# Attention scores in 64 by 64 tiles of TensorE, each block of queries with its own keys

## The chip, the cores and the metric

One core of one Trainium2 chip. The metric is device microseconds of one execution; a kernel is run several times and the median is given. The core has five engines that run side by side and meet at semaphores: TensorE (PE, whose weight loads the profile lists as PEld), VectorE (DVE), ScalarE (ACT), GpSimd (POOL) and SyncE (SP, which here issues the DMAs).

## The reference

Three stages follow each other: sparse attention, a gated feed-forward layer ("moe") and a second one ("moe2"). The change is in the attention. Four batches, eight heads, 512 local and 32 global positions, head size 64:

```
s_ll = scale * q_l @ k_l.T            # 512 x 512, kept where |i - j| <= 32
s_lg = scale * q_l @ k_g.T            # 512 x 32
a_l  = softmax([s_lg, s_ll])
out_l = a_l @ [v_g, v_l]
out_g = softmax(scale * q_g @ [k_g, k_l].T) @ [v_g, v_l]
x = [out_g, out_l] -> 2176 x 512 -> moe -> moe2
```

A local query sees 65 local keys and all 32 global ones.

## The kernel before

The attention stage is written out by hand. It is cut into small tasks, each with an engine (or two to choose from), the tasks it needs, and the PSUM banks it takes. `ORDER` is one long string; each letter names a kind of task in `KINDS`, and the next task of this kind is put there. A `+1` behind the kind chooses the second engine. So the string is the instruction order of all engines at once: on each engine tasks run in the order of the string, and an engine whose next task is not ready waits. `keep_busy` adds matmuls of zeros behind the first PE tasks, in numbers given by a string of digits (19 calls in all).

The tasks of a pair of heads `n` (16 pairs) are:

- `qk`: loads of keys and queries on SP. The queries are loaded shifted by 32 positions, so that a block of 64 queries has its keys in a window of 128.
- `A`: 16 transposes of 64 by 64 on PE (L212); `Ak` and `Aq` copy the turned keys and queries out of PSUM, to `kst` and `qT`, on ScalarE or DVE (L235, L237).
- `At` (L293, L294): POOL copies each pair of blocks' next 64 keys behind its own 128, so that row r of `kst` holds 192 local keys; `Ag` (L287): POOL copies the 32 global keys behind them, four times. A row has 224 keys.
- `S`, twice for a pair (g = 0, 1), so 32 calls of `scores` in the stage: four matmuls of 128 queries (two blocks of 64) and 224 keys, for two query pairs and two heads; the heads lie in the two halves of the partitions. L314.
- `M` (DVE, L325): adds the mask, writes the negated scores and their minimum; `E` (ScalarE, L332): the exponential and its sum; `R`, `N` (POOL, L344 and L346): the division. Eight of `M` and `E` a pair.
- `C`: transposes of the weights (L212), copied out by `V`; `D`: the product with the values (L378 with the global, L382 with the local ones), both for two heads in the two column halves of PE; `Xc`, `Xh`, `Xl`: the result is copied and split in a high and a low part.

For every two pairs there are global queries as well (`GA`, L408; `GT`; `GO`, L454), for every batch the turning of the global keys and queries (`AG`, L478, `AGk`, `AGe`, `GG`). Between them stand the first matmuls of the next layer (`F`, `F2`, L650) and the conversion of its first weights (`Cq`, `Cf`, `Ch`, `Cl`).

A PE matmul has a tile shape, the rows and columns of the array that it takes: 64 by 128 for the scores and the 64 by 64 transposes, 128 by 64 for `D`, `GA`, `GO` and `GG`, 128 by 128 for `AG`, `F`, `F2` and `keep_busy`.

Behind attention the two layers run from a list that a planner in the kernel puts in order when it is built; the change does not touch it.

Of the kernel before, what the change touches and what calls it, by code (L numbers as in the profile page):

```python
# [21 lines left out]
def tile_attn_moe_moe2(  # L22
# [69 lines left out]
    mask = e_p.tile([128, 224], F32, name="mask")  # L92
    mask7 = e_p.tile([128, 224], F32, name="mask7")
# [4 lines left out]
    def setup():  # L98
        nc.gpsimd.memset(ident, 1.0)
        nc.gpsimd.affine_select(out=ident, in_=ident, pattern=[[-1, 128]], compare_op=ALU.is_equal,  # L100
                                fill=0.0, base=0, channel_multiplier=1)
        keep_busy(0, 7)
        nc.vector.memset(qgbd, 0.0)
        for t in (vg, vgb):
            nc.vector.memset(t, 0.0)

        nc.gpsimd.memset(mask, 0.0)
        m = mask[:, 0:192]
        nc.gpsimd.affine_select(out=m, in_=m, pattern=[[1, 192]], compare_op=ALU.is_ge,
                                fill=NEG, base=0, channel_multiplier=-1)  # L110
        nc.gpsimd.affine_select(out=m, in_=m, pattern=[[-1, 192]], compare_op=ALU.is_ge,
                                fill=NEG, base=64, channel_multiplier=1)

        nc.gpsimd.tensor_copy(mask7, mask)
        nc.gpsimd.memset(mask7[64:96, 128:192], NEG)
        nc.gpsimd.memset(mask7[96:128, 64:128], NEG)


    XF = {}
# [90 lines left out]
    def transpose_half(out, src, j):  # L210
# [7 lines left out]
    KINDS = ("qk A gk w Ak+1 Aq At Cq AG AGk Ag S M E AGe GG GA GGe+1 Cf GM R vg v vgb N Ak GE GR GN C V "
             "Ch GT GV D AGk+1 Aq+1 GO Xc GXc+1 Xd GV+1 Cl Xc+1 GXh+1 Xh Xh+1 Xl GXl V+1 Ch+1 GXd F_v "
             "F_g GXc Ft Fg Fp Fh Fl Fh+1 GXl+1 F2 Fy Fy+1 GXh Xl+1").split()  # L220
    ORDER = "abcdaefgchaijkllmkmmmmmmnnnnibopedcnqgnramsnntbskfelfhluvammmmmmmmwnxnnngyybizgsAnBCkfDEDEnqsslmmFnnGcHm"
    ORDER += "muwnntlbnIemnnJAyayKmmmigDEDoBslkCEalpLkmmmmmnMnnumnGnnnmNmnnnIyywOwPbaQRDznESfOqDlsuyETUlmmmmmmmmnnnnyI"
    ORDER += "DDnrnnEngVVkWdtLXbwAlMefIusYZcmvOlmmQmgnUnnBbmmmM01ayymzhsnnf2DDnEEnCdqlssscgVGwnIUHamnmlummMVtnSAnyWyk1"
    ORDER += "YmmmmnnnnnUb0zxKOZaDXQiiDBlEjhul3Immm4kCyg1mmmmmVb5nnnnnnnnDsLefyEGwuoRTHl6DqEpy2lmOnmnmymnSgsbekkrfImmm"
    ORDER += "nnmDZwOadaE7nWns1tsYcDlgLEQVlmmAmmbInnnnu3eRmmyyqkmmKlUnn2D0wvVRBnEtDC4mmm00USWgVncm5GnuEhnnlOwy1s8xiHbd"
    ORDER += "7msmmyAnIefaDnnsmEn13nBCilsnMDjou0LyyEmmmml4wOGnnnngphmmmZkPrIDmw5Dnnnn0uEEbUlYssImeOMOmmmfUn2SqskyyVaDD"
    ORDER += "sZaELgEtlFQQlMImnnVkmmmm9TAnmBmmbVCnM2nnn!!xzufnnn#ylb!y!emmnnnSm#n6Km#gkwvwDDXX17gnZlOOddulmm$UIqWyymmm"
    ORDER += "mmmtGD1nnnnnnnnEu0P3ADVl45EL6lwIwmmnmnnmnyyBmmm7mNZnnnnDCuD!My!OREyXUGI%DU9PDEL$#X&VI2%9OMTOMUZ!!$$O&&"
# [36 lines left out]
    def add_pair(n):  # L265
# [14 lines left out]

        def kst():
            if (b, hp) not in KST:
                KST[b, hp] = kst_p.tile([128, 4, 224], F32, tag="kst", name="kst")
            return KST[b, hp]

        def glob_keys():
            nc.gpsimd.tensor_copy(kst()[:, :, 192:224], GK[b, "kT"][:, hp:hp + 1, :].to_broadcast([128, 4, SG]))  # L287

        def keys():
            duplicate(("Ak", n), kst()[:, :, 0:128].rearrange("c r (j t) -> c r j t", j=2), R["pk"])  # L290

        def more_keys():
            nc.gpsimd.tensor_copy(kst()[:, 0:3, 128:192], kst()[:, 1:4, 0:64])  # L293
            nc.gpsimd.tensor_copy(kst()[:, 3, 128:192], kst()[:, 0, 0:64])  # L294

        def queries():
            R["qT"] = qk_p.tile([128, 4, 128], F32, tag="qT", name="qT")
# [1 line left out]
            duplicate(("Aq", n), dst, R["pq"])  # L299

        task(("A", n), "PE", [("qk", n)], qk, 2, ("Aq", n))
        task(("Ag", n), "POOL", [("AGk", b), lastu("GA", n - 2), agog("S", 2, 1)], glob_keys)
        task(("Ak", n), "DVE ACT", [("A", n), lastu("GA", n - 2), agog("S", 2, 1)], keys)
        task(("At", n), "POOL", [("Ak", n)], more_keys)
        task(("Aq", n), "ACT DVE",
             [("A", n), ("Ak", n), agog("S", 2, 1)], queries)

        def scores(g):  # L310
            p = both(("S", n, g))
            for pp in range(2):
                for h in range(2):
                    nc.tensor.matmul(p[:, h, 224 * pp:224 * pp + 224], lhsT=R["qT"][half(h), 2 * g + pp, :],  # L314
                                     rhs=KST[b, hp][half(h), 2 * g + pp, :], start=True, stop=True)

        def minimum(g, i):
            if "sm" not in R:
                R["sm"] = sm_p.tile([128, NB, 224], F32, tag="sm", name="sm")
# [20 lines left out]
        def normalise(g):  # L340
            i0, i1 = 4 * g, 4 * g + 4
            r, sm = R["rc"][:, i0:i1], R["sm"]
            eng = nc.gpsimd if ON["N", n, g] == "POOL" else nc.vector
            eng.tensor_tensor(out=sm[:, i0:i1, 0:192], in0=sm[:, i0:i1, 0:192],  # L344
                              in1=r.unsqueeze(2).to_broadcast([128, 4, 192]), op=ALU.mult)
            eng.tensor_tensor(out=R["sng"][:, i0:i1, :], in0=sm[:, i0:i1, 192:224],  # L346
                              in1=r.unsqueeze(2).to_broadcast([128, 4, SG]), op=ALU.mult)


# [1 line left out]
        def turn(g):  # L351
            p = both(("C", n, g))
            for k in range(4):
                for j in range(2):
                    transpose_half(p[:, j, 64 * k:64 * k + 64], R["sm"][half(j), 4 * g + k, 64 * j:64 * j + 128], j)
# [6 lines left out]

        task(("R", n), "DVE", [("E", n, 0, 3), ("E", n, 1, 3)], reciprocal)
        for g in range(2):
            task(("S", n, g), "PE", [("Aq", n), ("At", n), ("Ag", n)], lambda g=g: scores(g), 2, ("M", n, g, 3))
            for i in range(4):
                task(("M", n, g, i), "DVE",
                     [("S", n, g), agog("C", 2, 1)], lambda g=g, i=i: minimum(g, i))
                task(("E", n, g, i), "ACT", [("M", n, g, i)], lambda g=g, i=i: exponential(g, i))
            task(("N", n, g), "POOL DVE", [("R", n), agog("C", 2, g)], lambda g=g: normalise(g))  # L370
            task(("C", n, g), "PE", [("N", n, g)], lambda g=g: turn(g), 2, ("V", n, g))
            task(("V", n, g), "ACT DVE", [("C", n, g), ago("D", 1)], lambda g=g: turned(g))
# [25 lines left out]
    def add_glob(u):  # L398
# [73 lines left out]
    def add_batch(b):  # L472
# [31 lines left out]
        task(("AGk", b), "DVE ACT", [("AG", b, 0)] + prev(("Ag", HP * b - 1), ("GG", b - 1)), keys)  # L504
# [32 lines left out]
    def attention():  # L537
# [903 lines left out]
```

## Time and profile before

| | |
|---|---|
| median of three runs | 891.6 us (891.56 to 893.38) |
| profiled execution, its own time | 890.72 us |
| span of its instructions | 889.0 us |
| PE busy | 877.6 us (99%) |
| VectorE, ScalarE, POOL busy | 649.6, 490.8, 541.3 us |
| attention ends on PE at | 158.8 us |

The profile is of one execution. A row of the timeline gives where instructions start, in microseconds from the start of the span, and how long one or several of them take; ends of matmuls are modelled, starts are recorded. The span leaves out what lies before the first and behind the last instruction, 1.7 us here.

### The profile page before, as it was taken

What the parts mean: (1) busy time and instruction counts of PE and PEld (TensorE: products, weight loads), DVE (VectorE), ACT (ScalarE), POOL (GpSimd) and SP (SyncE); (2) the same over time, 40 slices, a digit from 0 to 9 for tenths busy, and PEclk for the clock granted to TensorE, in tenths of its full rate; (3) what the DMA queues carried; (4) which work ended last, traced back from release to release, by engine and by line L of the source; (5) the groups of instructions that cost most, each with busy time, mean ns of one, the idle gap of its engine ahead of it and who ended that gap; (6) DMA issues with size and microseconds to landing.
All of it is one profiled execution on the core that took longest, in us unless ns stands there. A gap on an engine that the chain in (4) does not pass through costs nothing.

```text
span 889.0 us, 17205 instructions
## 1 busy us (share of the span) xinstructions
PE 877.6 (99%) x6252; PEld 808.0 (91%) x6252; DVE 649.6 (73%) x1224; ACT 490.8 (55%) x1177; POOL 541.3 (61%) x550
## 2 busy tenths in 40 slices
PE   7999999999999999999999999999999999999998
PEld 6777888988999999999999999998989898989896
DVE  5777786779777888778778899777777777753434
ACT  6888886454435454455455678764445444544341
POOL 4798887699964386375374799564454436633231
PEclk9999999999999999999999999999999999999999
DMA  7777775577555646646546335664737374726283
GB/s 167 169 182 168 189 173 147 197 233 240 195 190 197 224 148 209 205 139 230 178 153 221 137 142 194 224 222 156 250 116 261 121 263 139 259 80 197 61 266 144
DMA packets 165334, 164.19 MB, mean 185 GB/s; under 512 B 81793, under 2 KB 143745, under 8 KB 165249
## 3 DMA queue, kind: packets, MB, share of 16 engines
q1 hardware_dynamic: 163824, 162.24, 57.8%
q8 instruction: 49, 0.80, 0.4%
q10 hardware_dynamic: 1424, 0.85, 0.3%
q14 instruction: 37, 0.30, 0.1%
HBM read 136.31 MB, written 26.74 MB: 183 GB/s over the span
## 4 chain that ended last, share of the span: by engine, by line
PE 94%; DMA 2%; SPq 1%; DVE 1%; ACT 0%; issue 0%; ACTq 0%; DVEq 0%
PE p L1127 37%; PE p L1232 21%; PE p L1018 15%; PE p L1084 8%; PE one L650 3%; PE pair L212 2%; PE pair L314 2%; PE one L378 1%; PE one L382 1%; DMA qs<-in_q_l 1%; PE one L454 1%; DMA gkq<-in_q_g 1%; PE one L408 1%; DMA vw<-in_v_l 0%; SPq L178 0%
## 5 line engine op out<-in xcount | busy, mean ns | idle before, releaser
L1127 PE MATMUL p<-xh,w 128*128 128x384 f32 (+1 forms) x992 | 258.3, 326 | 0.0
L1232 PE MATMUL p<-w,a 128*128 128x512 f32 x816 | 194.3, 391 | 0.0
L1232 PEld LDWEIGHTS p<-w,a 128*128 128x128 f32 x816 | 152.2, 188 | 29.9
L1127 PEld LDWEIGHTS p<-xh,w 128*128 128x128 f32 x992 | 176.9, 188 | 1.4
L1127 PE MATMUL p<-xl,w 128*128 128x384 f32 (+1 forms) x496 | 161.5, 326 | 0.0
L1139 ACT ACTIVATE b<-p 128x384 f32<-128x384 f32 (+1 forms) x144 | 68.0, 472 | 158.1 <-PE p L1127 153.7
L1018 PE MATMUL p<-a,w 128*128 128x384 f32 (+2 forms) x768 | 142.8, 334 | 0.0
L1048 POOL TENSOR_TENSOR a<-b,a 128x384 fp32r<-128x384 f32 (+1 forms) x58 | 62.0, 1068 | 117.9 <-ACT a L1046 76.6
L1018 PEld LDWEIGHTS p<-a,w 128*128 128x128 f32 x768 | 130.5, 188 | 2.8
L1242 DVE TENSOR_TENSOR y<-p,y 128x512 f32<-128x512 f32 x119 | 82.1, 690 | 65.3 <-PE p L1232 63.8
L880 POOL TENSOR_TENSOR w<-cx,w 128x256 fp32r<-128x256 f32 (+1 forms) x90 | 100.0, 1119 | 44.4 <-ACT w L879 38.9
L833 DVE TENSOR_TENSOR b<-p,b 128x384 f32<-128x384 f32 (+1 forms) x144 | 76.3, 531 | 64.2 <-PE p L1127 42.9
L1048 POOL TENSOR_TENSOR a<-s,a 128x384 fp32r<-128x384 f32 (+2 forms) x53 | 61.5, 1161 | 65.8 <-ACT a L1046 65.8
L1127 PE MATMUL p<-e,w 128*128 128x384 f32 (+1 forms) x528 | 101.3, 328 | 0.0
L1127 PEld LDWEIGHTS p<-xl,w 128*128 128x128 f32 x496 | 93.1, 188 | 1.5
L1127 PEld LDWEIGHTS p<-e,w 128*128 128x128 f32 x528 | 90.0, 188 | 1.0
L1027 DVE TENSOR_TENSOR y<-p,y 128x384 f32<-128x384 f32 (+2 forms) x116 | 62.5, 542 | 22.7 <-PE p L1018 21.3
L1084 PE MATMUL p<-xh,w 128*128 128x384 f32 (+1 forms) x256 | 72.6, 355 | 0.0
L1046 ACT ACTIVATE a<-s 128x384 fp32r<-128x384 f32 (+2 forms) x88 | 45.4, 516 | 47.0 <-DVE s L1070 45.9
L591 DVE SCALAR_TENSOR_TENSOR fl<-q,st 128x512 f32<-128x512 f32 x68 | 62.4, 918 | 9.8 <-ACT q L583 9.6
L595 DVE SCALAR_TENSOR_TENSOR cx<-fl,cx 128x512 uint32<-128x512 uint32 x68 | 65.9, 969 | 0.5
L332 ACT ACTIVATE sm<-sm,nb 128x224 f32<-128x224 f32 x128 | 60.0, 473 | 3.7 <-DVE nb L325 3.6
(153 smaller groups left out, 1512.9 us busy)
## 6 DMA issues: line engine op xcount, KB each, us to landing
e<-td SPq DMA_DIRECT2D x76, 384.0 KB
xh<-td SPq DMA_DIRECT2D x38, 384.0 KB
xl<-td SPq DMA_DIRECT2D x38, 384.0 KB
st<-in_moe_w_out SPq DMA_DIRECT2D x28, 512.0 KB
st<-in_moe_w_in SPq DMA_DIRECT2D x16, 512.0 KB
vw<-in_v_l SPq DMA_DIRECT2D x32, 224.0 KB
e<-td SPq DMA_DIRECT2D x20, 320.0 KB
st<-in_moe_w_gate SPq DMA_DIRECT2D x12, 512.0 KB
```

The source lines that it names most:

```text
L591: nc.vector.scalar_tensor_tensor(fl, q, TINY2, hw, op0=ALU.is_ge, op1=ALU.mult)
L595: nc.vector.scalar_tensor_tensor(x, fu, 0xC0000000, x, op0=ALU.bitwise_and, op1=ALU.bitwise_or)
L833: return lambda e: vec(e).tensor_tensor(out=out(), in0=a(), in1=b(), op=op)
L880: add(lo or [("POOL", PO(n))], 0, lambda e: vec(e).tensor_tensor(out=dst(1), in0=src(), in1=dst(0).bitcast(F32), op=ALU.subtract), r=[rd, ...
L1018: nc.tensor.matmul(ps.h[:, 0:n], lhsT=a.h[:, d], rhs=b.h[:, at:at + n], start=(i == 0 and j == 0), stop=(i == len(ws) - 1 and j == 2))
L1027: add("DVE", DV(n), lambda e: nc.vector.tensor_tensor(out=ya, in0=ps.h[:, 0:n], in1=ya, op=ALU.add), r=[ps], w=yt)
L1048: t.append(add(either(n), 0, lambda e: vec(e).tensor_tensor(out=dst(1), in0=get(), in1=dst(0).bitcast(F32), op=ALU.subtract), r=[v, (av[0] ...
L1084: nc.tensor.matmul(ps.h[:, 0:n], lhsT=a.h[:, d], rhs=b[:, c, c0:c0 + n], start=(c == 0 and j == 0), stop=(c == KD - 1 and j == 2))
L1127: nc.tensor.matmul(ps.h[:, 0:n], lhsT=w.h[:, 256 * a + 128 * c:256 * a + 128 * c + 128], rhs=xs[b][:, c, :], start=(start and c == 0 and j ...
L1139: add("ACT", AC(n), lambda e: nc.scalar.activation(out=dst.h[:, 0:n], in_=src.h[:, 0:n], func=AF.Copy), r=[sv], w=[dst])
L1232: nc.tensor.matmul(ps.h, lhsT=a.h[:, d], rhs=b.h, start=(i == 0 and q == 0), stop=(i == len(ws) - 1 and q == 2))
L1242: add("DVE", DV(512), lambda e: nc.vector.tensor_tensor(out=ya, in0=pa(), in1=ya, op=ALU.add), r=[ps], w=tok)
```

## The change

The scores are computed for blocks of 64 queries, each with its own 128 local keys and the 32 global keys. `kst` holds the 512 local keys once; the copies `At` and `Ag` are gone, and the global keys are read from where `AGk` puts them, which now has two buffers. A call of `scores` has 16 matmuls instead of 4: 64 queries each, of 128 columns or of 32, and for the last block, whose window wraps, two of 64. The output rows of the two blocks lie in the two halves of the PSUM partitions as before. A row of scores has 160 columns instead of 224, and the masks, minimum, exponential and division follow it. The order string is a new one, with other engines chosen for some tasks: 11 of 32 `V` on DVE (6 before), 7 of 16 `Aq` on DVE (4 before), 1 of 8 `GV` on DVE (4 before), 3 of 32 `N` on DVE (none before), 6 of 16 `Xl` on DVE (3 before). `keep_busy` gets 18 calls. On SP the second half of a batch's first global load comes before the loads of pair 1.

```diff
         for j in range(2):
+            m = mask[half(j), 0:128]
+            nc.gpsimd.affine_select(out=m, in_=m, pattern=[[1, 128]], compare_op=ALU.is_ge,
+                                    fill=NEG, base=0, channel_multiplier=-1)
...
-                KST[b, hp] = kst_p.tile([128, 4, 224], F32, tag="kst", name="kst")
+                KST[b, hp] = kst_p.tile([128, SL], F32, tag="kst", name="kst")
...
-        def glob_keys():
-            nc.gpsimd.tensor_copy(kst()[:, :, 192:224], GK[b, "kT"][:, hp:hp + 1, :].to_broadcast([128, 4, SG]))
-
         def keys():
-            duplicate(("Ak", n), kst()[:, :, 0:128].rearrange("c r (j t) -> c r j t", j=2), R["pk"])
-
-        def more_keys():
-            nc.gpsimd.tensor_copy(kst()[:, 0:3, 128:192], kst()[:, 1:4, 0:64])
-            nc.gpsimd.tensor_copy(kst()[:, 3, 128:192], kst()[:, 0, 0:64])
+            duplicate(("Ak", n), kst().rearrange("c (r j t) -> c r j t", j=2, t=64), R["pk"])
...
-        task(("Ag", n), "POOL", [("AGk", b), lastu("GA", n - 2), agog("S", 2, 1)], glob_keys)
         task(("Ak", n), "DVE ACT", [("A", n), lastu("GA", n - 2), agog("S", 2, 1)], keys)
-        task(("At", n), "POOL", [("Ak", n)], more_keys)
...
         def scores(g):
-            p = both(("S", n, g))
+            p, keys = both(("S", n, g)), KST[b, hp]
             for pp in range(2):
-                for h in range(2):
-                    nc.tensor.matmul(p[:, h, 224 * pp:224 * pp + 224], lhsT=R["qT"][half(h), 2 * g + pp, :],
-                                     rhs=KST[b, hp][half(h), 2 * g + pp, :], start=True, stop=True)
+                r = 2 * g + pp
+                for j in range(2):
+                    i = 2 * r + j
+                    for c0, c1, o in ((64 * i, 64 * i + 128, 0),) if i < NB - 1 else ((SL - 64, SL, 0), (0, 64, 64)):
+                        for h in range(2):
+                            nc.tensor.matmul(p[half(j), h, 160 * pp + o:160 * pp + o + c1 - c0], lhsT=R["qT"][half(h), r, half(j)],
+                                             rhs=keys[half(h), c0:c1], start=True, stop=True)
+                    for h in range(2):
+                        nc.tensor.matmul(p[half(j), h, 160 * pp + 128:160 * pp + 160], lhsT=R["qT"][half(h), r, half(j)],
+                                         rhs=GK[b, "kT"][half(h), hp, :], start=True, stop=True)
...
-            eng.tensor_tensor(out=sm[:, i0:i1, 0:192], in0=sm[:, i0:i1, 0:192],
-                              in1=r.unsqueeze(2).to_broadcast([128, 4, 192]), op=ALU.mult)
+            eng.tensor_tensor(out=sm[:, i0:i1, 0:128], in0=sm[:, i0:i1, 0:128],
+                              in1=r.unsqueeze(2).to_broadcast([128, 4, 128]), op=ALU.mult)
...
-            task(("S", n, g), "PE", [("Aq", n), ("At", n), ("Ag", n)], lambda g=g: scores(g), 2, ("M", n, g, 3))
+            task(("S", n, g), "PE", [("Aq", n), ("Ak", n), ("AGk", b)], lambda g=g: scores(g), 2, ("M", n, g, 3))
...
-            kT = GK[b, "kT"] = g_p.tile([128, HP, SG], F32, tag="gkT", name="gkT")
+            kT = GK[b, "kT"] = g_p.tile([128, HP, SG], F32, tag="gkT", name="gkT", bufs=2)
...
-        steady = iter("040202002030020013")
+        steady = iter("030042000024201")
```

## Rows read from the trace of the kernel before

**Rows 1.** The page's busy times: microseconds, share of the span, instructions.

```profile
PE 877.6 (99%) x6252; PEld 808.0 (91%) x6252; DVE 649.6 (73%) x1224; ACT 490.8 (55%) x1177; POOL 541.3 (61%) x550
```

**Rows 2.** Busy time by stretch: stretch, length, PE, PEld, DVE, ACT, POOL, clock, DMA.

```profile
0.00:30.00 30.00, 25.07 (x284) 19.74 (x286) 17.49 (x75) 21.52 (x67) 16.04 (x40) 1.00 0.72 166
30.00:90.00 60.00, 57.32 (x928) 46.02 (x926) 45.34 (x176) 50.46 (x164) 51.85 (x65) 1.00 0.73 177
90.00:158.80 68.80, 68.80 (x1068) 58.61 (x1065) 51.30 (x173) 53.21 (x170) 53.90 (x63) 1.00 0.67 167
158.80:889.00 730.20, 726.37 (x3985) 683.67 (x3984) 535.45 (x802) 365.62 (x777) 419.49 (x385) 1.00 0.56 188
```

**Rows 3.** Busy time of `keep_busy` alone (L157) on PE and PEld, one stretch.

```profile
0.00:30.00 30.00, 9.62 (x52) 7.94 (x52) 1.00 0.72 166
```

**Rows 4.** The chain that ended last: start, length, what.

```profile
42.18 3.75 DMA vw<-in_v_l
```

**Rows 5.** Timeline of PE behind 125 us: start, length, instructions.

```profile
127.74 1.03 PE L314 MATMUL pair<-kst,qT 64*128 64x224 f32 x8
128.60 0.41 PE L212 MATMUL pair<-ident,ks 64*128 64x64 f32 x8
...
134.18 1.78 PE L314 MATMUL pair<-kst,qT 64*128 64x224 f32 x16
135.90 1.09 PE L378 MATMUL one<-pt,vg 128*64 128x128 f32 x16
136.82 1.10 PE L382 MATMUL one<-pt,vw 128*64 128x64 f32 x32
137.75 1.03 PE L408 MATMUL one<-kst,qgbd 128*64 128x512 f32 x4
...
142.13 0.97 PE L314 MATMUL pair<-kst,qT 64*128 64x224 f32 x8
143.03 0.66 PE L454 MATMUL one<-gtl,vw 128*64 128x32 f32 x16
143.52 0.29 PE L454 MATMUL one<-gtl,vgb 128*64 128x32 f32 x4
...
144.32 1.03 PE L314 MATMUL pair<-kst,qT 64*128 64x224 f32 x8
145.28 1.09 PE L378 MATMUL one<-pt,vg 128*64 128x128 f32 x16
```

**Rows 6.** Timeline of PE from 59.3 to 60.4 us.

```profile
59.48 0.28 PE L382 MATMUL one<-pt,vw 128*64 128x64 f32 x2
59.59 0.27 PE L378 MATMUL one<-pt,vg 128*64 128x128 f32 x1
59.60 1.02 PE L382 MATMUL one<-pt,vw 128*64 128x64 f32 x27
```

**Rows 7.** Groups by line and shape up to 150 us: busy, mean ns, idle before.

```profile
L332 ACT ACTIVATE sm<-sm,nb 128x224 f32<-128x224 f32 x128 | 60.0, 473 | 3.7 <-DVE nb L325 3.6
L344 POOL TENSOR_TENSOR sm<-sm,rc 128x768 f32<-128x768 f32 x31 | 46.8, 1510 | 11.2 <-DVE rc L338 8.0 <-ACT xf L235 2.4 <-ACT pt L235 0.9
L325 DVE CUSTOM_DVE_ANT_0 sm<-pair,mask 128x224 f32<-128x224 f32 x128 | 42.6, 385 | 21.4 <-PE pair L314 16.0 <-PE pair L212 1.7 <-POOL sng L346 1.7
...
L235 ACT ACTIVATE pt<-pair 128x640 f32<-128x640 f32 x25 | 17.1, 701 | 7.4 <-PE pair L212 6.6 <-ACT sm L332 0.6
...
L235 ACT ACTIVATE qT<-pair 128x512 f32<-128x512 f32 x12 | 7.1, 592 | 0.6 <-DVE kst L237 0.6
...
L293 POOL COPY kst<-kst 128x192 f32<-128x192 f32 x16 | 6.7, 419 | 10.6 <-ACT kst L235 9.6 <-DVE kst L237 1.0
```

**Rows 8.** Timeline of all engines from 5 to 9.3 us.

```profile
6.35 0.59 ACT L235 ACTIVATE qT<-pair 128x512 f32<-128x512 f32 x1
...
7.39 1.44 PEld L314 LDWEIGHTS pair<-kst,qT 64*128 64x128 f32 x16 [0.26 <-POOL kst L287]
...
7.83 1.15 SPq L169 DMA_DIRECT2D gkq<-in_q_g  x2
```

More of the change, by code (lines that the diff above doesn't have):

```diff
@@ L91, in tile_attn_moe_moe2 @@
     ident = e_p.tile([128, 128], F32, name="ident")
-    mask = e_p.tile([128, 224], F32, name="mask")
-    mask7 = e_p.tile([128, 224], F32, name="mask7")
+    mask = e_p.tile([128, 160], F32, name="mask")
+    mask7 = e_p.tile([128, 160], F32, name="mask7")
     qgbd = e_p.tile([128, HP, 2, SG], F32, name="qgbd")
@@ L107, in setup @@
         nc.gpsimd.memset(mask, 0.0)
[L108 to L112, printed above, removed]
+        for j in range(2):
+            m = mask[half(j), 0:128]
+            nc.gpsimd.affine_select(out=m, in_=m, pattern=[[1, 128]], compare_op=ALU.is_ge,
+                                    fill=NEG, base=0, channel_multiplier=-1)
+            nc.gpsimd.affine_select(out=m, in_=m, pattern=[[-1, 128]], compare_op=ALU.is_ge,
+                                    fill=NEG, base=64, channel_multiplier=1)
         nc.gpsimd.tensor_copy(mask7, mask)
-        nc.gpsimd.memset(mask7[64:96, 128:192], NEG)
-        nc.gpsimd.memset(mask7[96:128, 64:128], NEG)
+        nc.gpsimd.memset(mask7[64:96, 64:128], NEG)
+        nc.gpsimd.memset(mask7[96:128, 0:64], NEG)
     XF = {}
@@ L217, in tile_attn_moe_moe2 @@
     LETTERS = ascii_letters + digits + "!#$%&()*+-./:;<=>?@[]^_{|}~"
[L218 to L227, printed above, removed]
@@ L228, in tile_attn_moe_moe2 @@
-    ORDER += "mmmtGD1nnnnnnnnEu0P3ADVl45EL6lwIwmmnmnnmnyyBmmm7mNZnnnnDCuD!My!OREyXUGI%DU9PDEL$#X&VI2%9OMTOMUZ!!$$O&&"
+    KINDS = ("qk A Ak+1 gk AG AGk Aq S M w E Cq AGe Cf GA GG vg v GGe R N GM GE C V+1 vgb GR Ch+1 GN V D "
+             "Cl GT Aq+1 GV Xc+1 AGk+1 GO GXc+1 Ak Xh+1 Xl GXh GXl Xc Xd Ch GXd F_v F_g GXc GXh+1 Ft "
+             "GV+1 Fg Xh Fp Fh Fl GGe+1 F2 Xl+1 GXl+1 Fy Fy+1 Fh+1 N+1 Fl+1").split()
+    ORDER = "abcdefghijdahjiiiiikekdklkmakbnnnicogkhiepqrlnkkiiikshiibkkktiucvgakiiukwxyxzkABCDkhiiiihikrEFkkkbatinku"
@@ new lines, in tile_attn_moe_moe2 @@
+    ORDER += "kiicGkoHuktuuxIDxDJjdvhhiiiiwkkkkKaLAbiiiMNHCErreOxinxPykkkkDQGmRhInlbipiSTtEnucakHiihuOsikkxLUkyPTVixia"
+    ORDER += "oiFSyhbkkkkOtEiuciiiTgPrnukxhvWnqkSkOXiiniPDikYkkjxhyWiiddwiikZRkkhnrbtEikkkkuuNgTjzxiiAkioyVSxhCavklkeX"
+    ORDER += "DiiiKktehiuumkkGiE0wna1UFiLAkiikxYxCX2DybkkkSGnnntcrrXgIb3ThZc4PVpgoaiiluhiikkkksEiUuiiin5Txxa3DLnPDJhvk"
+    ORDER += "6RhkiiiiiEdFkkwktbiuqJkkkNiiAu0WXrgnCObYkxNeWDjHPd2kkxOznhTD4orkPitKiiuuEhiviV5iiiaxekkkkXDx6lmkGDWIQRhn"
+    ORDER += "nakkJkhiEw0iiiitBLiikkkikbrnuuxcAW2gnCDhMTV4kxXkTFDbriiiiBkOhkQptEa7iiiiukckFoSHGOxuI8aykk9!Sk#hxyLOkkTE"
@@ L230, in task @@
+    ORDER += "iiiivrkY9hkkjqbikk8ikStQuuNw8RzkAiHi#CXr$kbkxc8TVTDHOtPx%Ph#DWii6uhoikkkikiiiikkkE&0ktxvuuGDW2Ixw4jhLDAi"
+    ORDER += "ChkSiiiir5Ekkk(iiikMrxxkkky8JD8t&8TVTG&EI#$OOxxQyD!9L9EYZSS!8VTT39$$39"
     def task(name, engine, needs, work, banks=0, until=None):
@@ L310, in scores @@
         def scores(g):
-            p = both(("S", n, g))
+            p, keys = both(("S", n, g)), KST[b, hp]
             for pp in range(2):
-                for h in range(2):
-                    nc.tensor.matmul(p[:, h, 224 * pp:224 * pp + 224], lhsT=R["qT"][half(h), 2 * g + pp, :],
-                                     rhs=KST[b, hp][half(h), 2 * g + pp, :], start=True, stop=True)
+                r = 2 * g + pp
+                for j in range(2):
+                    i = 2 * r + j
[6 more added lines that the diff above has]
+                                         rhs=GK[b, "kT"][half(h), hp, :], start=True, stop=True)
         def minimum(g, i):
             if "sm" not in R:
-                R["sm"] = sm_p.tile([128, NB, 224], F32, tag="sm", name="sm")
+                R["sm"] = sm_p.tile([128, NB, 160], F32, tag="sm", name="sm")
                 R["sng"] = sm_p.tile([128, NB, SG], F32, tag="sng", name="sng")
@@ L325, in minimum @@
             nc.vector.tensor_tensor_reduce(
-                out=R["sm"][:, x], in0=both(("S", n, g))[:, h, 224 * pp:224 * pp + 224],
+                out=R["sm"][:, x], in0=both(("S", n, g))[:, h, 160 * pp:160 * pp + 160],
                 in1=mask7 if 2 * g + pp == 3 else mask, scale=-scale, scalar=3.0e38,
@@ L343, in normalise @@
             eng = nc.gpsimd if ON["N", n, g] == "POOL" else nc.vector
-            eng.tensor_tensor(out=sm[:, i0:i1, 0:192], in0=sm[:, i0:i1, 0:192],
-                              in1=r.unsqueeze(2).to_broadcast([128, 4, 192]), op=ALU.mult)
-            eng.tensor_tensor(out=R["sng"][:, i0:i1, :], in0=sm[:, i0:i1, 192:224],
+            eng.tensor_tensor(out=sm[:, i0:i1, 0:128], in0=sm[:, i0:i1, 0:128],
+                              in1=r.unsqueeze(2).to_broadcast([128, 4, 128]), op=ALU.mult)
+            eng.tensor_tensor(out=R["sng"][:, i0:i1, :], in0=sm[:, i0:i1, 128:160],
                               in1=r.unsqueeze(2).to_broadcast([128, 4, SG]), op=ALU.mult)
@@ L354, in turn @@
                 for j in range(2):
-                    transpose_half(p[:, j, 64 * k:64 * k + 64], R["sm"][half(j), 4 * g + k, 64 * j:64 * j + 128], j)
+                    transpose_half(p[:, j, 64 * k:64 * k + 64], R["sm"][half(j), 4 * g + k, 0:128], j)
             for j in range(2):
@@ L407, in scores @@
                 lq = qgbd[:, 2 * up + e].rearrange("c h r -> c (h r)")
-                nc.tensor.matmul(one(("GA", u))[half(e)], lhsT=lq, rhs=KST[b, 2 * up + e][:, :, 0:128],
+                nc.tensor.matmul(one(("GA", u))[half(e)], lhsT=lq, rhs=KST[b, 2 * up + e],
                                  start=True, stop=True)
@@ L503, in add_batch @@
         task(("AG", b, 0), "PE", [("gk", b, 0)], lambda: turn(0), 1, ("AGe", b))
-        task(("AGk", b), "DVE ACT", [("AG", b, 0)] + prev(("Ag", HP * b - 1), ("GG", b - 1)), keys)
+        task(("AGk", b), "DVE ACT", [("AG", b, 0)] + ([("S", HP * (b - 1) - 1, 1), ("GG", b - 2)] if b > 1 else []), keys)
         task(("AG", b, 1), "PE", [("gk", b, 1), ("AG", b, 0)], lambda: turn(1))
```

## The prediction

> **What bounds the kernel now.** I read the page's busy times first. TensorE is busy 99% of the span and no other engine reaches 75% [rows 1]. That is an average over two stages, so the second view is the table of stretches [rows 2]. The change touches only the attention stage, which ends at 158.8 us. In the stage behind it PE is busy 726.37 of 730.20 us in code that stays as it is; it will start earlier or later and keep its length. Inside attention there are three parts. Up to 30 us PE is idle for 4.93 us, and 9.62 us of its busy time are the dummy matmuls of `keep_busy` [rows 2, 3]; that is a ramp in which ScalarE (21.52 of 30 us) and the loads set the pace. From 30 to 90 us PE idles 2.68 us. From 90 us on it does not idle at all. So whatever the new score matmuls cost more or less on PE is paid in full behind 90 us, and nearly so before; whatever the other engines gain counts only up to 90 us. [...] The third view is the chain that ended last: before 90 us it leaves PE for loads, for instance 3.75 us for a value window at 42.18 us [rows 4], so not every idle microsecond is an engine's fault.
>
> **What a score call costs on PE.** The timeline of PE gives starts [rows 5]. An f32 matmul leaves two records, so `scores(g)` with four matmuls is a group of 8. The group of 16 takes 135.90 - 134.18 = 1.72 us to the next group, the group of 8 takes 145.28 - 144.32 = 0.96; both come from and go to another tile shape. The difference, 0.76 us, is one body without its edges: 4 pairs of records of 224 columns, 0.19 us a pair, the two heads side by side in the two row halves. Edges: the group of 8 at 127.74 goes on to transposes, which have its own shape (64 rows by 128 columns), and takes 0.86, so leaving for another shape costs 0.10; the one at 142.13 comes from transposes and takes 0.90, so entering from another shape costs 0.06.
>
> Rates of 64-column weights stand in the same rows: 16 records of 128 columns in 136.82 - 135.90 = 0.92 us, less the 0.05 of entering 0.109 a pair; 32 records of 64 columns in 137.75 - 136.82 = 0.93 us, 0.058 a pair; 16 records of 32 columns in 143.52 - 143.03 = 0.49 us, 0.061 a pair. So 32 columns cost what 64 do, which counts against the separate matmul over 32 global keys.
>
> **The new body.** A call now has 16 matmuls, 32 records: for each of two query pairs and each half j, two passes over 128 local columns and two over 32 global ones, for both heads. One half's passes take 2 x 0.109 + 2 x 0.058 = 0.334 us. No row shows a 64 by 64 tile, so this is bounded from both sides. If the four tiles run at once, j = 0 and j = 1 overlap and a call takes 2 x 0.334 = 0.668, which is 0.088 less than now, 32 times: -2.8 us. If the halves run one behind the other it takes 1.336: +18.6 us. The row nearest to the question is at 59.48 us [rows 6]: the two column halves of the output matmuls had got out of step, and one half starts L382 at 59.48, 0.11 us before the other half starts its last L378, though all of L378 is written ahead of L382. So the column halves have queues of their own and pass each other; the row halves run side by side in [rows 5]. A 64 by 64 tile is both at once, and I take 0.668. [...]
>
> **Edges.** Transposes share the present shape and nothing shares the new one. Decoding both order strings and putting the dummy matmuls where the digits put them, PE changes shape 106 times in attention now and 121 times then. 15 x (0.10 + 0.06) = +2.4 us; entering with weights half as wide may be cheaper, so +1.5 is the lower end. Body and edges together: -0.4 us. The fewer columns are paid back in edges.
>
> **The other engines.** The two key copies and the copy of the global keys leave POOL (the largest, L293, is 6.7 us in all), normalising shrinks from 768 to 512 columns at 1510 ns, and 3 of 32 normalisations go to DVE [rows 7]. POOL is not on the chain, so that is nothing by itself, except at the very start: the first scores wait for the last of those copies until 7.39 us, while the queries, which they still need, are there at 6.35 + 0.59 = 6.94 [rows 8]. -0.45 us. The masks' extra two selects on POOL lie in its idle time ahead of the first copy. On ScalarE copies of 640 and 512 columns take 701 and 592 ns, 0.85 ns a column, so an exponential over 64 columns fewer loses 0.054 of its 473 ns [rows 7]. In the ramp ScalarE is the engine with the least room, and it takes about 24 exponentials there (three pairs): -1.3 us; none if loads pace it, -2.0 if waits shorten too. DVE's minimum (385 ns) loses columns too, but the order gives DVE five more of the copies behind C and three more of the query copies (and three fewer behind GT); I count nothing for it. The dummy matmuls go from 19 to 18 calls: -0.2. Between 30 and 90 us I give back half of the 2.68 us of idle time, -1.3 (bounds: none, all), because scores no longer wait for POOL and ScalarE has some 4 us less to do there.
>
> The new order moves loads on SP: the second half of the global load now stands ahead of pair 1's keys and queries, and that is 1.15 us of issue [rows 8]. Pair 1 comes later by as much; behind it wait its transposes on PE and its two copies on ScalarE, which is still at pair 0's exponentials then. I count it as covered; without that cover the gain of the start is gone and 0.7 us with it. The second buffer for the turned global keys lets a batch's keys be copied before the last batch's scores are done; it removes a wait and adds none.
>
> **Sum.** -2.8 + 2.4 - 0.45 - 1.3 - 0.2 - 1.3 = -3.65 us. The profiled execution took 890.72 us (span 889.0), so 887.1; the median of the runs stands 0.9 above it, so 888.0.
>
> **Rivals.**
> *One start per 29 ns.* The fastest sustained rate in the trace is 32 records of 64 columns in 0.93 us, and those of 32 columns are no faster [rows 5]. If that is what PE can hand out in all, and not what each tile's weight load takes, a call of 32 records takes 0.93 us: 0.26 above the 0.668 of the sum, 8.4 us over 32 calls, so 888.0 + 8.4 = 896.4. For it: no row is faster over a stretch. Against it: at 59.59 and 59.60 us the two halves start 0.01 us apart [rows 6]. A queue with little room, full of one half's second passes before the other half is reached, ends at about the same body. [...]
>
> *The halves in turn.* The body is 1.336 us, 888.0 + 21.4 = 909.4, a little less where PE still idled. This is the rival of the other sign at its full price. It decides early: above 0.78 us a call (0.756 + 0.85 / 32) nothing of the gain is left. Against it speaks [rows 6].
>
> *Loads hide the gain.* The chain before 90 us passes through loads, and DMA is busy 0.72 and 0.73 of the time there [rows 2, 4]. Then ScalarE's and the idle time's terms and the dummy call give nothing: 888.0 + 2.8 = 890.8, no change.
>
> **Chances and range.** The forecast has 0.53, loads hiding it 0.12, the limit of starts 0.20, the halves in turn 0.15. Its own range is 885 (all of the idle time, cheap edges) to 890.5. The limit of starts spreads from 892 to 900 with a queue between the two bodies. 884.5 to 902 leaves out the halves in turn and little else. About 0.2% (1.8 us) is what a measurement of this kernel can tell from no change. Faster by more 0.50 (most of the forecast), within it 0.14, slower 0.36 (both PE rivals and a bit).
>
> **What would show it.** In the changed kernel's PE timeline one score group from and to other shapes should take 0.668 + 0.16 = 0.83 us to the next start, a double one 1.50; 1.09 would be the limit of starts, 1.50 for a single one the halves in turn. The first scores start at 6.9 to 7.0 us; attention ends near 155 us; PE idles under 6 us before 90 us and not behind; POOL's copies are gone and nothing waits for them. The stretch from there to the end keeps its 730 us. The forecast fails if a score group takes more than 0.94 us, if shape changes cost more with the new shape than 0.16, or if the early idle time stays where it is.

## The result, and the profile of the changed kernel

The changed kernel takes 897.33 us (median of 8 runs, 893.82 to 901.61) against 891.72 of the kernel before on the same chip: 1.0062, interval 1.0041 to 1.0082. It is 5.6 us slower where 3.65 less was forecast, inside the range and on the wrong side. The profiled execution has a span of 894.9 us, 5.9 more than before.

The page's busy times of the changed kernel: microseconds, share of the span, instructions.

```profile
PE 876.8 (98%) x7082; PEld 811.5 (91%) x7082; DVE 643.9 (72%) x1243; ACT 481.8 (54%) x1168; POOL 503.7 (56%) x494
```

PE is busy for 0.8 us less than in [rows 1], with 830 matmul records more. Busy time by stretch, columns as in [rows 2]:

```profile
0.00:30.00 30.00, 25.42 (x435) 20.96 (x435) 17.12 (x77) 18.88 (x65) 12.13 (x30) 1.00 0.67 156
30.00:90.00 60.00, 55.16 (x1295) 46.66 (x1292) 41.63 (x175) 46.07 (x160) 36.44 (x41) 1.00 0.72 176
90.00:164.70 74.70, 69.85 (x1378) 60.19 (x1377) 48.24 (x189) 51.19 (x170) 35.74 (x40) 1.00 0.63 157
164.70:894.90 730.20, 726.36 (x3985) 683.68 (x3984) 536.95 (x804) 365.69 (x777) 419.36 (x385) 1.00 0.57 188
```

Attention ends at 164.70 in place of 158.80, and the stretch behind keeps its 730.20 us, so the whole difference lies in attention. There PE is busy for 150.43 us (151.19 in [rows 2]) and idle for 4.58 + 4.84 + 4.85 = 14.27 us (7.61). The new waiting is behind 30 us: 2.16 us more up to 90, and 4.85 where there was none.

The score groups on PE's timeline, one from and to other shapes and one double:

```profile
86.40 0.46 PE L310 MATMUL pair<-kst,qT 64*64 64x128 f32 x8
...
87.90 1.09 PE L377 MATMUL one<-pt,vg 128*64 128x128 f32 x16
...
97.45 0.46 PE L310 MATMUL pair<-kst,qT 64*64 64x128 f32 x8
97.72 0.28 PE L313 MATMUL pair<-gkT,qT 64*64 64x32 f32 x8
97.81 0.45 PE L310 MATMUL pair<-kst,qT 64*64 64x128 f32 x8
98.06 0.29 PE L313 MATMUL pair<-gkT,qT 64*64 64x32 f32 x8
98.28 0.65 PE L407 MATMUL one<-kst,qgbd 128*64 128x512 f32 x2
```

A single group takes 98.28 - 97.45 = 0.83 us, a double one 87.90 - 86.40 = 1.50: the two figures forecast. Four tiles do run at once. What PE waits for, 30 to 90 us and then behind 90 us (in total, times, longest):

```profile
PE pair L213 <- DMA qs<-in_q_l: 2.3, 2, 1.4
PE one L477 <- DMA gkq<-in_q_g: 0.8, 1, 0.8
...
PE one L649 <- ACT xf L236: 2.3, 1, 2.3
PE one L477 <- DMA gkq<-in_k_g: 1.1, 1, 1.1
PE pair L213 <- DMA qs<-in_q_l: 0.7, 1, 0.7
PE one L477 <- DMA gkq<-in_q_g: 0.6, 1, 0.6
```

The longest are loads, but for one, and that on `xf` is a transfer too: ScalarE's copy waits for a store, that is, for a buffer that the store gives back. ScalarE's longest wait of this kind behind 90 us, and three pieces of the chain that ended last:

```profile
ACT xf L236 <- DMA xf<-xf: 4.2, 2, 2.9
...
47.78 3.63 DMA qs<-in_q_l
...
117.76 4.50 DMA xf<-xf
130.59 3.04 DMA xf<-xf
```

The queue that issues them is SyncE's, of which [rows 8] have a single row. Its timeline, in a stretch of the changed kernel:

```profile
101.07 0.40 SPq L138 DMA_DIRECT2D xf<-xf  x1
101.57 1.28 SPq L203 DMA_DIRECT2D vw<-in_v_l  x2
102.90 2.29 SPq L204 DMA_DIRECT2D vw<-in_v_l  x1
105.24 0.63 SPq L205 DMA_DIRECT2D vw<-in_v_l  x1
105.98 0.52 SPq L138 DMA_DIRECT2D xf<-gxf  x1
106.60 1.14 SPq L179 DMA_DIRECT2D ks<-in_k_l  x2
107.85 2.52 SPq L181 DMA_DIRECT2D qs<-in_q_l  x2
```

From 4 us to 144 it has no gap of more than 0.53 us: one issue, mostly of 0.4 to 0.6 us, stands behind the other. But of the twin loads L204 and L205, equal in size, one takes 2.29 us and the other 0.63, and the two of L181 take 2.52 together. Such issues beyond 0.9 us are 25 of the 224 in attention here and 16 in the kernel before. They stand where PE's instructions are fetched. The page lists those fetches as a DMA queue of its own (packets, MB, share); in attention the changed kernel has

```profile
q8 instruction: 24, 0.39, 1.1%
```

and the kernel before

```profile
q8 instruction: 18, 0.29, 0.8%
```

They are packets of 16 KB (16384 bytes each, 0.92 MB in 56). In the whole execution there are 56 of them to 7082 matmul and 7082 weight-load records of PE, 253 records to a packet; in the kernel before it was 49 to twice 6252, 255; the 256 of the expectations below is within 1.2% of both. Of the 24 in attention, 22 overlap an issue of over 0.9 us, and 23 of the 25 such issues overlap one; the 33 issues at a fetch take 1.15 us in the mean, the other 191 take 0.51; in the kernel before it is 29 at 0.90 and 195 at 0.51 (each worked out from all records of the trace, with the packets on the clock of the DMA view). That they are fetches for PE is read from these counts, and from e9 and e15 below, where they go from 18 to 24 with 1536 more of its instructions and from 24 to 20 with 1152 fewer.

**Theories.** (A) *Fetches*: the many small matmuls bring six fetches more; each holds up SyncE's gapless list by the better part of a microsecond; loads and stores land later and PE waits. (B) *Order*: the tiles gain what was forecast, and the new written order loses it. (C) *The tiles themselves cost*, outside their own body.

### The profile page after: what moved, and what is told of

Same layout as the page of the kernel before. It is cut to its first block, busy times and chain, and to the rows that moved or that the text cites. A ratio compares the mean times of both kernels' runs of the same rounds, so it can differ in the third digit from the quotient of the medians.

```text
span 894.9 us, 18831 instructions
## 1 busy us (share of the span) xinstructions
PE 876.8 (98%) x7082; PEld 811.5 (91%) x7082; DVE 643.9 (72%) x1243; ACT 481.8 (54%) x1168; POOL 503.7 (56%) x494
## 3 DMA queue, kind: packets, MB, share of 16 engines
q1 hardware_dynamic: 163824, 162.24, 57.6%
## 4 chain that ended last, share of the span: by engine, by line
PE 91%; DMA 3%; SPq 3%; DVE 1%; issue 0%; ACT 0%; DVEq 0%; ACTq 0%
PE p L1126 37%; PE p L1231 21%; PE p L1017 15%; PE p L1083 8%; PE one L649 3%; PE pair L213 2%; DMA qs<-in_q_l 1%; PE pair L310 1%; PE one L377 1%; PE one L381 1%; DMA xf<-xf 1%; DMA gkq<-in_q_g 1%; PE one L453 1%; SPq L181 1%; SPq L179 1%
## 5 line engine op out<-in xcount | busy, mean ns | idle before, releaser
L596 DVE SCALAR_TENSOR_TENSOR cx<-st,cx 128x512 uint32<-128x512 uint32 x68 | 60.3, 889 | 0.4
```

## Experiments

Each is held against the kernel before, run beside it on the same chip (medians 891.27, 891.03, 892.37 and 891.37 us in four groups).

**e1, the tiles in the old order.** The changed kernel with `KINDS`, `ORDER` and digits of the kernel before, less the letters of `Ag` and `At`.

> The 64 by 64 tiles and the narrower masks, normalisation and minimum as changed, but the written order (and the dummy matmuls' digits) of the kernel before, with the two POOL copy tasks dropped from it. Theory 'order': the tiles gain what was forecast and the new order lost it, so 888 to 890 us, attention ending near 156 us. Theory 'instruction fetches': PE has some 800 more matmul records in attention and as many weight loads, which are about 6 more fetches of 256 instructions, and each holds SyncE's DMA issue up by about 1 us; the loads come 6 to 9 us late again and the time is 895 to 898, with 23 to 24 fetches and over 20 issues longer than 0.9 us before the end of attention.

896.56 us, 1.0046 (1.0026 to 1.0066). Theory B falls as the main cause: without its order the change loses 5.3 us (4.1 by the ratio). As the order is the old one, SyncE's list is the same as before, transfer by transfer, and can be compared row by row. The last load of the first layer's weights in attention, in the kernel before:

```profile
133.57 1.00 SPq L579 DMA_DIRECT2D st<-in_moe_w_gate  x2
```

and in e1:

```profile
143.28 1.80 SPq L578 DMA_DIRECT2D st<-in_moe_w_gate  x2
```

9.7 us later, with 24 fetches in place of 18 and 22 issues beyond 0.9 us ahead of this row in place of 15. The lateness is in the issues themselves: SyncE's first 209 (again from all records) take 128.8 us together against 117.3, and the gaps between them do not grow (15.0 and 16.0). Those that overlap a fetch went from 23.0 us (25 issues) to 36.7 (30), the others from 94.3 to 92.1. e1 pays in two ways. PE is idle for 11.0 us in attention (3.4 more than before). And its granted clock fell: over ten microseconds in which PE was busy for 7.89 its mean was 1.00, and over the next ten it was 0.66.

```profile
10.00:20.00 10.00, 7.89 (x163) 6.20 (x155) 6.68 (x41) 8.56 (x33) 2.75 (x4) 1.00 0.69 168
20.00:30.00 10.00, 9.79 (x131) 6.92 (x131) 4.62 (x17) 5.94 (x22) 2.83 (x2) 0.66 0.59 132
```

If PE's work goes with its clock, 9.79 us at 0.66 do that of 6.5, and by this estimate 3.3 us went there; busy time in attention is 154.5 us against 151.2, 3.3 more. What brought the clock down is not shown: the kernel before was busy for 8.00 us of the same ten and kept it.

**e2, the order with the old scores.** The kernel before with the new string; `At` and `Ag` stand behind `Ak`.

> The kernel before (224-column score matmuls, key copies on POOL) with the new written order and digits; the POOL copies stand right behind the turned keys. Theory 'order': the loss is the order's, so 897 or more. Theory 'instruction fetches': PE has no more instructions than before, 18 fetches in attention, so 890 to 893, unless the POOL copies that the order knows nothing of cost something.

893.47 us, 1.0023 (1.0012 to 1.0033): 2.2 us, a little above what theory A gave. 18 fetches, as many as before; PE's added waits are for POOL (L344, 2.7 us; the global keys' copy L287, 2.0), for whose copies this order has no room. So what the order costs is a small part, and partly the test's own.

**e3, wide scores cut in three.**

```diff
-                    nc.tensor.matmul(p[:, h, 224 * pp:224 * pp + 224], ...
+                for c0, c1 in ((0, 75), (75, 150), (150, 224)):
+                    nc.tensor.matmul(p[:, h, 224 * pp + c0:224 * pp + c1], ...
```

> The kernel before with nothing changed but that each score matmul of 224 columns is written as three of 75, 75 and 74, in the same row tiles: the same columns, 512 more matmul records and as many weight loads, about 4 more fetches. By the rate of 128 columns a pair of records (0.109 us) the body is 12 x 0.064 = 0.77 against 0.756 us, +0.3 us in all. Theory 'order' (or any cost of the 64 by 64 shape): 892.0, no change. Theory 'instruction fetches': SyncE's list is 4 to 5 us later and the kernel 893.5 to 896.

901.53 us, 1.0121 (1.0105 to 1.0138), above both expectations and no test of A, since PE itself became slower. The expectation's price was wrong:

```profile
120.42 1.51 PE L315 MATMUL pair<-kst,qT 64*128 64x75 f32 x24
121.87 1.09 PE L379 MATMUL one<-pt,vg 128*64 128x128 f32 x16
```

A call takes 1.45 us; less the edges' 0.16 that is 0.108 us for each of its 12 pairs, what a pair of 128 columns took in [rows 5], there with weights of 128 by 64. PE was busy for 165.9 us of attention, and behind 90 us it did not wait: a slower PE gives SyncE's list its time.

**e4, stores issued by ScalarE.** In the changed kernel `nc.scalar.dma_start` for the 24 stores to `xf`.

> The changed kernel with its 24 stores of x (tasks Xd and GXd) issued by ScalarE in place of SyncE: SyncE's list loses 24 issues of some 0.45 us, 11 us, and ScalarE gains them. The bytes are the same. Theories 'instruction fetches' and any other in which SyncE's issuing is what runs late: PE's added 6.7 us of waiting go, 888 to 891 us. Theory 'order' in the sense that DMA bytes or PE's sequence set the waits, not SyncE's list: 895 to 898.

903.15 us, 1.0127 (1.0113 to 1.0142), above both expectations. SyncE's list got room, but ScalarE stood still at its own stores, for which the profile names transfers of SyncE's (waits of ScalarE: in total, times, longest):

```profile
ACT pt L236 <- DMA vw<-in_v_l: 7.4, 2, 5.5
```

PE then waited 4.0 us at once for ScalarE's `pt`. Nothing follows for A.

**e5, e6, e7, few value windows.** In `load_v`, for the changed kernel (e5), the kernel before (e6) and the tiles in the old order (e7):

```diff
+        n = b * HP + hp
+        if n > 1:
+            VW[b, hp] = VW[0, n % 2]
+            return
```

> The changed kernel, in which only the first two head pairs' value windows are loaded and the other fourteen pairs use those again: 56 of SyncE's 224 issues, some 30 us of its list, and 3.6 MB are left out (so the values of the other pairs are not the reference's); PE's work is the same. To be held against e6, the kernel before with the same left out. Theory 'late loads' (the tiles gain on PE what was forecast, and SyncE's list, held up by more instruction fetches, takes it back): 3 to 4 us below e6, with PE idle under 1 us behind 30 us. Theory 'the tiles themselves cost' (or the clock falls whenever PE waits, for whatever reason): 3 us or more above e6, as with all loads.

> The kernel before with the value windows of the first two pairs alone, as in e5. PE was idle for 7.6 us in attention and some 3 us of it behind 30 us: 887 to 890 by either theory.

> The 64 by 64 tiles in the old written order (e1) with the value windows of the first two pairs alone. Against e6 this is the tiles alone with room on SyncE's list. Theory 'late loads': 2 to 4 us below e6. Theory 'the tiles themselves cost': 4 to 5 us above e6, as e1 stood above the kernel before.

887.33 us (e5), 887.32 (e6), 887.86 (e7): 0.9953 (0.9933 to 0.9973), 0.9950 (0.9935 to 0.9965) and 0.9960 (0.9946 to 0.9973) of the kernel before with all loads. The changed kernel gains some 10 us from this room, the kernel before 4, and the difference between them is gone. That speaks against C and for late loads. It does not tell issues from bytes: the 56 issues left out carried 7.3 MB (162.24 MB of SyncE's transfers in the whole execution of the changed kernel, 154.89 in e5), twice what the expectation says. e5's profile up to 150 us:

```profile
0.00:30.00 30.00, 25.88 (x485) 21.45 (x487) 17.77 (x79) 20.38 (x68) 13.63 (x32) 1.00 0.72 168
30.00:90.00 60.00, 58.20 (x1308) 49.41 (x1301) 44.57 (x183) 47.88 (x167) 39.70 (x44) 1.00 0.56 145
90.00:150.00 60.00, 60.00 (x1259) 52.06 (x1259) 41.51 (x174) 45.94 (x155) 30.94 (x35) 1.00 0.35 94
```

Behind 90 us PE waits no more; 1.8 us are left between 30 and 90, where I had expected under 1 us in all. And the 3 to 4 us below e6 that I expected are not there, nor the 2 to 4 of e7. The two profiled executions (clock 1.00) have spans of 883.5 and 885.7 us, 2.2 apart; the medians are equal, and the two longest of e5's five runs are those with a mean clock under 0.997.

**e8 and e12, stores issued by GpSimd**, in the changed kernel and in the kernel before.

```diff
-            nc.sync.dma_start(out=xf[:, kd:kd + nk, c0:c0 + n], in_=src)
+            nc.gpsimd.dma_start(out=xf[:, kd:kd + nk, c0:c0 + n], in_=src)
```

> The changed kernel with its 24 stores of x issued by GpSimd: 24 issues (11 us) leave SyncE's list, the bytes stay, ScalarE is not touched (in e4 it stood still at its own stores). GpSimd is busy for half of attention. Theory 'late loads': 889 to 893. If transfers themselves, not SyncE's list, are late, or if GpSimd's issuing holds up the normalisation: 897 or more.

> The kernel before with its 24 stores alone on GpSimd, as in e8. SyncE's list loses 11 us but PE waited behind 30 us for only 2.7: 888.5 to 891.5, a gain of 0 to 2.5 against e8's gain of 6.8 on the changed kernel.

e8: 890.49 us, 0.9992 (0.9980 to 1.0004), 6.8 below the changed kernel (6.2 by the ratios) with the same bytes in the same written order. So room on SyncE's list gives the loss back. (The stores also go through another queue here, so by this run alone the transfers are not ruled out.) e12: 901.98 us, 1.0104 (1.0087 to 1.0121), a miss. On GpSimd a store that waits for its source holds up what stands behind it (9.8 us in three waits here), and both the key copies and the stores wait for ScalarE (waits of GpSimd in e12):

```profile
POOL kst L293 <- ACT kst L235: 10.6, 3, 5.9
...
POOL xf L137 <- ACT xf L235: 9.8, 3, 4.6
```

Whether it is the key copies or the written order that leaves no room here is not shown: e16 below has the old order without the copies, and loses as well.

**e9, empty instructions on PE.** In the kernel before, behind each score matmul:

```diff
+                    for _ in range(12):
+                        nc.tensor.nop(hint="pad", nofuse=True)
```

> The kernel before with 12 empty instructions on PE behind each score matmul: 1536, 6 fetches of 256 more, no data and no column more. Theory 'instruction fetches': 24 fetches in attention, 5 or more issues of SyncE beyond 0.9 us more than the 16 of before, SyncE's list 5 to 9 us later at the same transfer (the tiles in the old order were 9.7 us late at the 200th), and 893 to 897 us. If PE's queue pays for the empty instructions itself, that shows as busy or unreleased time on PE and not as waits for loads. Rival (fetches are harmless, the tiles or the narrower work on the other engines shift the list): 891 to 892, SyncE's list as before.

980.7 us, 1.0984 (1.0964 to 1.1004), far above both expectations. 24 fetches came, as counted, but attention became longer by (248.75 - 158.81) us / 1536 = 59 ns for each empty instruction, part of it at a lower clock (0.73 from 30 to 90 us):

```profile
30.00:90.00 60.00, 54.23 (x549) 39.06 (x546) 24.55 (x103) 29.90 (x96) 29.04 (x37) 0.73 0.41 99
```

With a PE as slow as that SyncE's list has time to spare: it waited 68.8 us for PE's L456 alone. So the time says nothing on A. The issues do: the 25 at a fetch took 0.87 us in the mean, the other 199 took 0.50, with no 64 by 64 tile in the kernel.

**e10 and e11, early value loads on GpSimd as well**, for the kernel before and the changed one: e8's stores, the value windows of pairs 0 and 1 and the first batch's global values.

> The kernel before with its 24 stores, the value windows of the first two pairs and the first batch's global values (13 loads) issued by GpSimd: 37 of 224 issues, some 19 us, leave SyncE's list. Theory 'late loads': PE's 2.7 us of idle time behind 30 us and some of the ramp go, 887 to 890. GpSimd is busier here (121.8 us of attention) than in the changed kernel, so its own issues may cost up to 2 us back.

> The changed kernel with the same 37 issues on GpSimd. Theory 'late loads' (the tiles gain 1.5 to 4 us on PE once loads are there): 885 to 888.5, below e10 by 1 to 3, with PE idle for less than 7 us in attention. If the early value windows take transfer time from the first keys and queries instead: 890 or more.

920.98 us, 1.0321 (1.0299 to 1.0342), and 900.79 us, 1.0097 (1.0079 to 1.0115): both missed. A value window issued by GpSimd stands behind up to 4.6 us for which the profile shows no releaser (timeline of GpSimd, e11):

```profile
10.78 0.98 POOL L206 DMA_DIRECT2D vw<-in_v_l  x1 [4.52 <-issue]
16.39 0.95 POOL L206 DMA_DIRECT2D vw<-in_v_l  x1 [4.63 <-issue]
20.45 0.64 POOL L207 DMA_DIRECT2D vw<-in_v_l  x1 [3.11 <-issue]
...
32.09 0.98 POOL L206 DMA_DIRECT2D vw<-in_v_l  x1 [3.21 <-issue]
```

and the divisions behind it start late: PE waits 8.0 us for POOL's `sm` in e11, 17.3 in e10. What it is that GpSimd waits for stays open.

**e15, fewer instructions at nearly equal PE time.** The run that tells A apart.

```diff
-                    for c0, c1, o in ((64 * i, 64 * i + 128, 0),) if i < NB - 1 else ...
...
+                    c0 = min(64 * i, SL - 192)
+                    for h in range(2):
+                        nc.tensor.matmul(p[half(j), h, 160 * pp:160 * pp + 192], lhsT=R["qT"][half(h), r, half(j)],
+                                         rhs=keys[half(h), c0:c0 + 192], start=True, stop=True)
```

> The changed kernel, in which each half's local and global matmul is one matmul of 192 columns (so the last columns' scores are others than the reference's): 9 matmuls a pair and half fewer on average, 1153 instructions of PE or 4.5 fetches fewer, with the tiles, the written order, SyncE's list and PE's time kept (2 x 0.163 against 2 x 0.167 us a query pair, 0.5 us in all). Theory 'instruction fetches': some 20 fetches in attention, SyncE's list 4 to 5 us earlier at the same transfer, and 892 to 894.5. Rival (the fetches are harmless and the list is late for another reason): 896.5 to 897.5, the list as late as now.

891.82 us, 1.0002 (0.9992 to 1.0012): the loss is gone. PE's time for the scores is nearly the same:

```profile
83.46 1.53 PE L310 MATMUL pair<-kst,qT 64*64 64x192 f32 x32
84.92 1.09 PE L374 MATMUL one<-pt,vg 128*64 128x128 f32 x16
...
94.88 0.88 PE L310 MATMUL pair<-kst,qT 64*64 64x192 f32 x16
95.69 1.08 PE L404 MATMUL one<-kst,qgbd 128*64 128x512 f32 x4
```

0.81 and 1.46 us a group, 0.02 and 0.04 less than above, 0.6 us over 32 calls. There are four fetches fewer,

```profile
q8 instruction: 20, 0.33, 0.9%
```

17 issues beyond 0.9 us in place of 25, and the same load of weights is issued at 143.54 us in the changed kernel

```profile
143.54 0.43 SPq L578 DMA_DIRECT2D st<-in_moe_w_gate  x1
```

and 8.3 us earlier here:

```profile
135.26 0.43 SPq L575 DMA_DIRECT2D st<-in_moe_w_gate  x1
```

That is more than the 4 to 5 us expected. The 209 issues ahead of this row, the same in both kernels and in the same sequence, take 128.0 us together in the changed kernel and 118.6 here; the gaps come to 14.8 and 15.8 us. Of the 9.3 us, 8.1 are in issues that overlap a fetch (21 fetches there and 31 issues with 36.6 us, 16 and 30 with 28.6 here). Tiles, written order, loads and bytes are those of the changed kernel; PE's idle time in attention falls from 14.3 to 8.6 us. (The scores no longer read the turned global keys here, but in the changed kernel no wait of PE's is for these.) So the instructions cause the loss, 5.5 of the 5.6 us (5.3 by the ratios), and SyncE's issues at the fetches are where the list loses its time. Less is shown of where PE gets it back: in the profiled executions its idle time falls by 2.1 us up to 30 us, by 1.7 up to 90 and by 1.8 behind. Of the 7.0 us of new waiting behind 30 us, 3.5 are still there, behind 90 us for ScalarE's `xf` (1.9 us) and a load of global keys (1.1 us), and why stays open. Nor does the forecast gain appear here.

**e13, e14, e16, room on SyncE's list.** e13 is e8, e14 the kernel before and e16 is e1 with the stores on GpSimd, each with the second pair's query loads on ScalarE as well:

```diff
-        eng = nc.sync if b or hp else nc.scalar
+        eng = nc.sync if b or hp > 1 else nc.scalar
```

> The changed kernel with its 24 stores on GpSimd (e8) and, besides, the second pair's four query loads issued by ScalarE at the start, as the first pair's are. That takes another 2 us off SyncE's list ahead of every later load. In e8 PE waited 9.9 us in the first 90 us, most of it for loads. Theory 'late loads': 2 to 3 us below e8, 887.5 to 889.5, below the kernel before. If the ramp is held by ScalarE instead (four issues of 0.5 us stand in front of its copies): e8's 890.5 or more.

> The kernel before with the second pair's four query loads on ScalarE, nothing else. PE waited 4.9 us in the first 30 us and 2.7 in the next 60: 889 to 891.5 by 'late loads', no change or 1 us more if ScalarE holds the ramp.

> The 64 by 64 tiles in the old written order (e1, 896.6) with the 24 stores on GpSimd and the second pair's query loads on ScalarE. SyncE's list loses some 13 us. Theory 'late loads': e1's wait and clock losses go, 887 to 890. If the old order has no room on GpSimd for the stores without the key copies (as e12 had none with them): 893 or more.

e13: 889.20 us, 0.9976 (0.9965 to 0.9987), the fastest full kernel here, 2.2 us below the kernel before. e14: 891.72 us, 1.0002 (0.9993 to 1.0012); the same loads moved give the kernel before nothing. e16: 899.02 us, 1.0081 (1.0062 to 1.0101), a miss: its mean granted clock was 0.89 over the first 30 us, and PE waited for ScalarE's `xf`, `qT` and DVE's `gtl`. That the old order has stores and copies at places that do not suit GpSimd is likely and not shown. e13 up to 150 us:

```profile
0.00:30.00 30.00, 25.77 (x485) 21.25 (x486) 17.78 (x79) 20.39 (x68) 13.65 (x32) 1.00 0.72 168
30.00:90.00 60.00, 55.73 (x1271) 47.04 (x1264) 43.77 (x179) 46.05 (x161) 42.49 (x51) 1.00 0.76 183
90.00:150.00 60.00, 60.00 (x1205) 51.72 (x1204) 43.42 (x175) 45.37 (x156) 41.79 (x49) 1.00 0.72 176
```

The waiting behind 90 us is gone though there are 24 fetches; the list has 28 issues fewer. Between 30 and 90 us 4.27 us of it are left.

## Why the prediction was wrong

- *The body* (0.668 us, four tiles at once) was right to 0.01 us, and with it the weighing of both rivals on PE: neither the limit of starts (1.09 a group) nor halves in turn (1.50) came. The lower end of the limit's spread, 892 us, stands for 0.79 us a call ((892 - 888.0) / 32 + 0.668), a limit that no run shows; 0.67 was measured.
- *Body, edges and dummy calls* were put at -2.8 + 2.4 - 0.2 = -0.6 us; PE's busy time in attention fell by 0.8. That it agrees so well is partly luck: with the same matmuls, at a granted clock of 1.00, PE was busy for 148.0 us in e13 and 147.4 in e5, against 150.4 in the changed kernel.
- *First scores* at 7.25 us, not 6.9 to 7.0: 0.14 of the 0.45 us came; the copy of the queries, which [rows 8] has at 6.35, started at 6.46 and ended at 7.05. *The exponentials in the ramp* (-1.3): each exponential did shrink as priced, from 473 to 420 ns, but idle time up to 30 us fell by 0.35 in all.
- **The step that failed** is the change's cost on SyncE, which the sum puts at nothing. The prediction weighed there only which loads changed places ("I count it as covered") and gave back half of PE's idle time from 30 to 90 us. It priced 16 matmuls in place of 4 as time on PE, and not as instructions that have to be fetched. In place of -1.3 us between 30 and 90 the runs showed +2.2, and in place of 0 behind 90 us +4.85; e15 gives 5.5 us back by taking 1152 instructions away (576 records of matmuls and as many of weight loads). PE was to idle under 6 us before 90 us and not behind; it did so for 9.4 and 4.85. How much of the waiting that e15 leaves belongs to the new order stays open.
- What lay under it was a reading of [rows 2]: that PE does not idle behind 90 us was taken as a bound on PE alone. It was nearly a draw. From 4 us to 134.6 SyncE's list had no gap of more than 0.57 us either, so it could not make up for longer issues. Only then did it have a reserve, a wait of 9.1 us for a buffer that PE's L454 gives back. In the changed kernel the list comes to this point at 144.0 us, and its gap is 5.8 us long. SyncE's longest wait up to 158.8 us in the kernel before (in total, times, longest):

```profile
SPq L202 <- PE one L454: 9.5, 2, 9.1
```

- *The rival "loads hide the gain"* named the right place. Its price, no change, was the least that this mechanism could cost, because it kept the loads where they were.
- *The gain itself*: e13, with stores and loads moved, is 2.2 us below the kernel before; in the few-value runs the medians of e5 and e6 are equal and the profiled executions 2.2 apart. All of this is less than 3.65. That a part is lost to the clock is likely from e1 and e5 and not shown by itself.

## What to carry to other kernels

Before cutting wide matmuls into narrow ones, count PE's instructions as well as its columns: some 255 more were one more fetch, and a fetch went with 33 x 0.64 / 24 = 0.9 us of longer issues in the changed kernel (29 x 0.39 / 18 = 0.6 in the kernel before). Look for the queue without gaps on its own timeline; no busy table lists it, and a stage in which PE never waits may have no reserve in it (SyncE's list in the kernel before: no gap above 0.57 us from 4 to 134.6 us). Issues moved to another engine take part in that engine's order: the same 24 stores on GpSimd gave 6.8 us in the changed kernel and cost 9.6 in the kernel before.

## What the runs showed of the hardware that was not expected

- A fetch of PE's instructions (16 KB) goes with a longer issue on SyncE where the two meet: 1.15 us an issue at a fetch against 0.51 elsewhere in the changed kernel, 0.90 against 0.51 in the kernel before, 0.87 against 0.50 in e9, where 1536 of the instructions are empty. What these issues wait for is not shown by any run.
- An empty instruction on PE among 224-column matmuls costs 59 ns in the mean, idle time and the lower clock that came with it (0.73 from 30 to 90 us) included (e9).
- 75 columns with weights of 64 by 128 took 0.108 us a pair (e3), as long as 128 columns with weights of 128 by 64 (0.109, [rows 5]). The four 64 by 64 tiles, where half of the matmuls have 32 columns, got a start every (0.83 - 0.16) us / 32 = 21 ns, faster than the fastest sustained rate read in the kernel before (29 ns).
- Four of GpSimd's loads of value windows stand behind 3.1 to 4.6 us without a releaser (e11), while its 24 stores took 0.5 to 0.8 us each, and the waits in front of them have releasers (e8).
